# Other rooms and another order for loads and sums in a Fourier-mixing kernel on one core: y's stage, MLP2's begin, chunk 0 and the tail

## The chip, the cores and the metric

The kernel runs on one core of one Trainium2 chip. The metric is device time in microseconds for one execution of the whole program. An execution is also profiled, and the profile gives the start and length of every instruction on each engine: PE (matmuls), PEld (weight loads of PE), DVE (vector), ACT (scalar), POOL and SP, of which SP and POOL here do nothing but start transfers.

## The reference

Four products in a row, all in fp32, on x of 2048 x 512:

```python
xn = _layernorm(x, axis=-1)
a = einsum("bsd,ed->bse", xn, dft_hid_re);  b = einsum("bsd,ed->bse", xn, dft_hid_im)
s = einsum("ts,bse->bte", dft_seq_re, a) - einsum("ts,bse->bte", dft_seq_im, b)
h = einsum("bsd,df->bsf", xn, w1) + b1;  h = relu(h) ** 2
g = silu(einsum("bsf,fd->bsd", h, w2) + b2)
return x + s * g
```

The two Fourier products are made in the other order than written: first along the sequence, then along the hidden dimension.

## The kernel before, in words

**Numbers.** Each fp32 operand is split into a high and a low part: `split_hi` (line 133) on ACT rounds it, `split_lo` (line 136) on DVE subtracts the high part. A product takes three passes of matmuls (`PASSES`): high by high, high by low, low by high. Most products use a scheme of Strassen's kind with seven block products instead of eight. For that, sums of blocks have to be made on DVE before an operand is split (`sums_b`, `sums_a`, `sums_rows`, lines 281 to 299), and results are combined afterwards. An operand so prepared has seven blocks, so one `split_hi` or `split_lo` handles 1792 columns.

**Stages.** They follow one another in PE's order:

- *Chunk 0 and chunk 1* (loops at lines 508 and 560) multiply the normalized x by 256 columns each of the sequence matrices, without the seven-block scheme (`products`, line 367). Each has eight steps j of 24 matmuls of 512 columns. In chunk 0, step j also normalizes the tokens of x_j: statistics (`ln_stats`, `ln_var`), the normalized rows (`ln_xn`) and their split into `xc`. x_j is loaded by `load_x` (line 195), into the room `pq{j // 2 % 2}{j % 2}`.
- *Chunks 2 to 7* (line 593) use the seven-block scheme on x too. Its sums are `sums(g)` (line 245, four instructions on DVE for half of x) and `split_sums` (line 257). They are made aside, in chunk 1: the list `aside` (line 538) holds all these pieces and the first two operands of the hidden matrices, `d0` and `d1`, each piece with a rough cost. `beside(spent)` (line 542) takes pieces from that list in every step of chunk 1 until the cost reaches `ASIDE`.
- *y's stage* (lines 920 and 953) multiplies the result, which lies in DRAM, by the hidden matrices. Its 16 operands are loaded (`y_load`, line 424), summed (`y_sums`) and split (`y_split`). Eight units of two operands each; `Y_SIDE` (line 51) lists what else is made beside each unit.
- *MLP1* (line 995) makes h in 28 units of 84 matmuls; `H_SIDE` (line 63) says what is prepared beside each, among it the first operands of MLP2.
- *MLP2* (line 1037) has 28 steps n = 7 c + p of 42 matmuls of 256 columns. Step n needs the operand `h{n}` (`operand`, line 714) and the weights W2[p]. Each is made in three calls of `go`: load, sums, split. `O_SIDE` (line 94) lists what is called beside the regular calls in the first steps.
- *The tail* (line 1098 on) is the end of MLP2's last part: the products are ordered by block, each output block goes through `silu`, `times` (by s), `plus` (x) or `add_x` (a transfer that adds x), and out.

**What orders the work.** Each engine runs its instructions in the order in which the program lists them; the order above is written out by hand. An engine waits at an instruction until what it needs is there, and all behind it on that engine waits too. SP's queue is the same: a load that waits for its room holds up all loads behind it.

**Rooms.** `buf(tag, ...)` (line 168) gives a tile in a named room. A new tile in a room waits until the last reader of the old one is done. `u` has three rooms that are used in turn; `e`, `wd0`, `wd1` and `pq00` to `pq11` have one each. In MLP1, `wd0` holds W1[6], and `e` holds raw parts of W2. `make_w2` (line 695) loads w6 into `e`; `operand` loads h4, like every fourth, into `wd0`.

**The tail's banks.** C21's last product (k = 4) is made in two halves, in two banks `m4`, after what has to be subtracted was subtracted inside the bank. So only `silu`, `times` and `plus` follow the last matmul. C12's last product (k = 3) is made whole before it.

Of the kernel before, what the change touches and what calls it, by code (L numbers as in the profile page):

```python
# [13 lines left out]
P = 128  # L14
# [7 lines left out]
WARM = 8, 6  # L22
PLAIN = 2

ASIDE = 4.2

REST = NP - 4

# [56 lines left out]
    21: ((), ("h1",), ("w2",)),  # L85
    22: ((), ("h0", "w1"), ()),
    23: ((), ("h1",), ("w3",)),
    24: ((), ("w1",), ("w6", "h2")),
    25: ((), ("w2",), ("h3", "l4")),
    26: ((), ("w2", "w3"), ("l5",)),  # L90
    27: ((), ("w3", "h2"), ()),
}
ACT_PAIR = (4, 6, 8, 10, 12, 14, 16, 18, 21, 25)
O_SIDE = {0: (("h4", "w6"), ("h5",)), 1: ((), ("w6",))}

EPS = 1e-5
HI, LO = 0, 1
# [31 lines left out]
def fnet_gated_kernel(ctx, tc, x, xt, ct, wd, w1, w2, b1, b2, out):  # L129
# [6 lines left out]
    def split_lo(hi, lo, src):  # L136
        nc.vector.tensor_tensor(lo, src, hi.bitcast(F32), op=ALU.subtract)  # L137
# [52 lines left out]
        XC[j] = operand_buf(f"xc{j}", f"xc{j}", 3 if j in TURNED else 1, (7, 2, 256))  # L190
    small = buf("e", [P, 3, 16], "small")

    xr, xn32 = {}, {}

    def load_x(j, hs=slice(0, 2)):

        if j not in xr:
            xr[j] = buf(f"pq{j // 2 % 2}{j % 2}", [P, 2, D], f"x{j}")
        nc.sync.dma_start(xr[j][:, hs], x.rearrange("(h j p) d -> j p h d", h=2, p=P)[j][:, hs])

    def ln_stats(j, h=0):
# [216 lines left out]
        nc.sync.dma_start(x_, PQD[n // 2][:, n % 2])  # L418

    Y_HOME = ("xc3", "xc0"), ("xc4", "xc5"), ("xc6", "xc7")  # L420
    YFIRST = 3
    yop, yraw, WDP = {}, {}, {}

    def y_load(n):
        if n < 2 * NC:
            yraw[n] = buf("u", [P, 8, 256], f"yraw{n}")
            load_pq(n, yraw[n][:, 4:8])

    def y_sums(n):
# [73 lines left out]
    split_hi(*g)  # L503
    for h in range(2):
        products(0, 0, h)
    load_c(0, 3)
    load_x(4)
    for j in range(1, NJ):
        ln_rstd(j)
        for h in range(2):  # L510
            ln_xn(j, h)
            split_hi(*xc_parts(j, h))
        split_lo(*g)
        load_c(*order[j + 3])
        if j + 4 < NJ:
            load_x(j + 4)
        split_lo(*xc_parts(j, 0))
        if j + 1 < NJ:
            ln_stats(j + 1)
            ln_mean(j + 1, 1)  # L520
            ln_var(j + 1, 1)
            ln_root(j + 1)
        split_lo(*xc_parts(j, 1))
        for h in range(2):
            products(0, j, h)
        g = plain_parts(*order[j + 1])
        split_hi(*g)
        if j == 2:
            nc.sync.dma_start(b1s, b1)
            nc.sync.dma_start(b2s, bcast(b2, D))  # L530
    split_lo(*g)


    def run(*names):
        go(*names)
        return 1.6

    aside = chain(sums(0), (split_sums(j) for j in range(ND)), sums(1), (split_sums(j) for j in range(ND, NJ)),
                  (run(v) for v in ("d0", "d0", "d0", "d1", "d1", "d1")))
    accs.append([bank(tag, f"pq1_{tag}") for tag in ("b30", "b31", "b32", "ba")])  # L540

    def beside(spent):
# [9 lines left out]

    plain_out(0)
    plain_out(1)
    beside(0)
    plain_out(2)
    plain_out(3)
    for k in range(2):
# [1 line left out]
    for j in range(NJ - 1):  # L560
        if j == NJ - 4:
            go("d2")
        split(*plain_parts(1, j + 1))
        if j == NJ - 2:
            step_sums(0)
            go("d2")
        load_c(*order[NJ + j + 4])
        if j == 1:
            go("d0", "d1")
        for h in range(2):  # L570
            products(1, j, h)
        beside(split_s1(j - 1) if j else 0)
# [122 lines left out]
    def make_w2(p):  # L695
        if p in (2, 3):
            r, t = (buf(f"pq{p - 2}{i}", [P, 4, 256], f"w2raw{p}_{i}") for i in range(2))
        else:
            e = buf("e", [P, 8, 256], f"w2raw{p}")
            r, t = e[:, 0:4], e[:, 4:8]  # L700
        nc.sync.dma_start(r, w2[p])
        yield
        sums_b(t, r)
        yield
        g = operand_buf(W2_HOME[0 if p in W2_LATE else p], f"w2_{p}", 0)
        for q, src in ((slice(0, 3), r[:, 1:4]), (slice(3, 7), t)) if p in (2, 3) else ((slice(0, 7), e[:, 1:8]),):
            split(g[:, HI, q], g[:, LO, q], src)
        if p in W2_LATE:
            nc.sync.dma_start(W2D[p], g.bitcast(F32))
        else:  # L710
            W2[p] = g
        yield

    def operand(n):

        apart = n in (0, 1, 3)
        if apart:
            x_, t = (buf(f"pq{n % 3}{i}", [P, 4, 256], f"hr{n}_{i}") for i in range(2))
        else:
            e = buf("u" if n % 4 else "wd0", [P, 8, 256], f"hr{n}")  # L720
            x_, t = e[:, 4:8], e[:, 0:4]
        nc.sync.dma_start(x_, HD[divmod(n, NP)])
        yield
        sums_rows(t, x_)
        yield
        g = ready[n] = operand_buf("wd0" if n == NTC * NP - 1 else ("xc6", "xc7", "xc4")[n % 3], f"g{n}", 1)
        for s, src in ((slice(0, 4), t), (slice(4, 7), x_[:, 0:3])) if apart else ((slice(0, 7), e[:, 0:7]),):
            split(g[:, HI, s], g[:, LO, s], src)
        yield
# [190 lines left out]
    for u in range(2):  # L920
        unit = YUnit(u)
        unit.products(1)
        unit.seed("B", "A")
        if u:
            y_split(4)
            y_load(7)
        unit.products(7)
        unit.m7()
        unit.products(6)
        unit.seed("C", "B")  # L930
        y_split(3 + 2 * u, split_hi)
# [12 lines left out]
        if u:  # L944
            y_split(6, split_hi)
        unit.products(3)
        unit.c12()
        if not u:
            y_sums(4)
            y_sums(5)  # L950
    y_sums(7)
    before = None
    for u in range(2, NC):
        n = 2 * u + 2
        unit = YUnit(u)
# [81 lines left out]
    for n in range(NTC * NP):  # L1037
# [74 lines left out]
    silu(e, C11)  # L1112
    for f in (tail - 1, tail):
        rest((6, 7), (f,))
    step(C12, ms[6], C21, ALU.add)
    times(c, e, C11)
    add_x(c, e, C11)
    step(C21, ms[7], C12, ALU.subtract)
    rest((5,), (tail - 1, tail))
    for i in range(2):  # L1120
        nc.vector.tensor_tensor(m4[i][:, w[i]], m4[i][:, w[i]], e[:, C21, w[i]], op=ALU.subtract)
    step(C22, ms[5], C21, ALU.add)
    silu(e, C22)
    step(C12, ms[5], C12, ALU.subtract)
    times(c, e, C22)
    plus(c, e, C22)
    rest((3,))
    put(c, e, C11)
    step(C12, ms[3], C12, ALU.add)
    silu(e, C12)  # L1130
    times(c, e, C12)
    plus(c, e, C12)
    for i, part_ in enumerate((one, two)):
        for f in range(REST, NP):
            outer(m4[i], 4, NP * c + f, (i,))
        nc.scalar.activation(e[:, C21, w[i]], m4[i][:, w[i]], AF.Silu)
        times(c, e, C21, part_)
        plus(c, e, C21, part_)


def _launch(arrays, out_shape):
# [40 lines left out]
```

## Time and profile before

| | us |
|---|---|
| three timed runs | 675.19, 675.82, 680.76 |
| median | 675.82 |
| the profiled execution | 674.92 |
| its span | 673.1 |
| PE busy | 666.6 |
| DVE busy | 597.4 |
| ACT busy | 378.3 |

The span runs from the program's first instruction to its last; the execution's time is 1.8 us longer. A line of a timeline gives start and length in us, engine, line, operation, output and input tile, shape and count; a bracket is the idle time of the engine just before, and what ended it. A row of the windows gives the bounds and length of a stretch, the busy time (and count) of PE, PEld, DVE, ACT and POOL in it, PE's granted clock, and the share and rate of the DMA engines. PE's granted clock is 1.00 wherever a row is shown below.

### The profile page before, as it was taken

The numbers are of one execution on the slowest core, as the hardware profiler recorded it, in microseconds if no ns is written. First come the engines' busy times: TensorE is split into PE (matmuls) and PEld (weight loads), VectorE is DVE, ScalarE is ACT, GpSimd is POOL, SyncE is SP. The second block draws the span as 40 slices with busy tenths as digits, with TensorE's granted clock in tenths as the row PEclk, the third lists the DMA queues.
The fourth block names the chain that finished last, engine by engine and source line by source line (L and its number), as shares of the span: only waits on it lengthen the run. The fifth ranks groups of instructions, "written<-read, shape, count | busy, mean of one in ns | idle before, by whom it ended". The sixth has DMA issues, their size and how long they took to land.

```text
span 673.1 us, 13176 instructions
## 1 busy us (share of the span) xinstructions
PE 666.6 (99%) x5438; PEld 646.9 (96%) x5438; DVE 597.4 (89%) x830; ACT 378.3 (56%) x523; POOL 8.8 (1%) x11
## 2 busy tenths in 40 slices
PE   9999999999999999999999999999999999999997
PEld 6888789999999999999999999999999999999996
DVE  7979888999999999799899989887878789999996
ACT  6845654634444454444465458778778855454451
POOL 0000000000000000000000000000000000101010
PEclk9999999999999999999999999999999999999999
DMA  8635677646556775659588658574856956777775
GB/s 302 215 118 195 214 283 270 218 143 220 203 174 218 258 274 174 249 186 352 187 263 281 218 175 327 190 282 172 298 167 194 349 207 211 190 218 202 209 214 142
DMA packets 51723, 150.82 MB, mean 224 GB/s; under 512 B 4944, under 2 KB 19536, under 8 KB 50256
## 3 DMA queue, kind: packets, MB, share of 16 engines
q1 hardware_dynamic: 43552, 129.28, 56.6%
q10 hardware_dynamic: 6208, 18.88, 7.1%
q0 software_dynamic: 1904, 1.84, 1.9%
q8 instruction: 42, 0.69, 0.4%
q14 instruction: 17, 0.14, 0.1%
HBM read 101.98 MB, written 47.99 MB: 223 GB/s over the span
## 4 chain that ended last, share of the span: by engine, by line
PE 95%; DVE 2%; DMA 2%; issue 0%; ACT 0%; DVEq 0%
PE m L361 34%; PE r_B L752 13%; PE m_o L858 12%; PE r_A L752 9%; PE pq_b L376 8%; PE r_C L752 4%; PE r_D L752 4%; PE m_last L858 4%; PE pq_ba L376 2%; PE pq_bc L376 2%; PE pq_bb L376 2%; DMA hr<-hd 1%; PE warm L482 1%; DVE g L137 0%; DMA out<-z 0%
## 5 line engine op out<-in xcount | busy, mean ns | idle before, releaser
L361 PEld LDWEIGHTS m<-g,xc 128*128 128x128 f32 x2016 | 228.7, 188 | 0.1
L361 PE MATMUL m<-g,xc 128*128 128x256 f32 x2016 | 228.7, 276 | 0.0
L134 ACT ACTIVATE g<-u 128x1792 fp32r<-128x1792 f32 (+2 forms) x65 | 99.0, 1523 | 126.9 <-PE m L361 97.9
L137 DVE TENSOR_TENSOR g<-u,g 128x1792 fp32r<-128x1792 f32 (+2 forms) x65 | 116.8, 1797 | 20.0 <-ACT g L134 19.4
L858 PE MATMUL m_o<-w,g 128*128 128x256 f32 x882 | 101.3, 277 | 0.3 <-DVE g L137 0.2
L858 PEld LDWEIGHTS m_o<-w,g 128*128 128x128 f32 x882 | 100.6, 188 | 0.7 <-DVE g L137 0.7
L134 ACT ACTIVATE g<-hr 128x1792 fp32r<-128x1792 f32 (+2 forms) x31 | 48.1, 1563 | 42.4 <-DVE hr L295 21.0
L752 PE MATMUL r_B<-xT,w 128*128 128x256 f32 x504 | 66.5, 276 | 0.0
L376 PE MATMUL pq_b<-g,xc 128*128 128x512 f32 x240 | 65.6, 392 | 0.0
L752 PEld LDWEIGHTS r_B<-xT,w 128*128 128x128 f32 x504 | 61.4, 188 | 0.0
L137 DVE TENSOR_TENSOR g<-hr,g 128x1792 fp32r<-128x1792 f32 (+2 forms) x31 | 56.7, 1838 | 2.9 <-ACT g L134 2.8
L376 PEld LDWEIGHTS pq_b<-g,xc 128*128 128x128 f32 x240 | 44.7, 188 | 10.8 <-DVE g L137 0.8
L752 PE MATMUL r_A<-xT,w 128*128 128x256 f32 x336 | 42.8, 276 | 0.0
L752 PEld LDWEIGHTS r_A<-xT,w 128*128 128x128 f32 x336 | 40.2, 188 | 0.0
L752 PE MATMUL r_B<-wdp,yg 128*128 128x256 f32 x288 | 35.9, 277 | 0.0
L283 DVE TENSOR_TENSOR u<-u 128x512 f32<-128x512 f32 x48 | 32.9, 685 | 3.1 <-DMA u<-in_ct 3.1
L752 PEld LDWEIGHTS r_B<-wdp,yg 128*128 128x128 f32 x288 | 34.1, 188 | 0.1
L858 PE MATMUL m_last<-w,g 128*128 128x256 f32 x294 | 33.5, 276 | 0.0
L858 PEld LDWEIGHTS m_last<-w,g 128*128 128x128 f32 x294 | 33.4, 188 | 0.0
L137 DVE TENSOR_TENSOR yg<-yraw,yg 128x1792 fp32r<-128x1792 f32 x13 | 26.1, 2017 | 0.3 <-ACT yg L134 0.3
L134 ACT ACTIVATE yg<-yraw 128x1792 fp32r<-128x1792 f32 x13 | 22.2, 1711 | 7.2 <-DVE yraw L292 7.2
L752 PE MATMUL r_D<-xT,w 128*128 128x256 f32 x168 | 23.6, 276 | 0.0
(186 smaller groups left out, 878.0 us busy)
## 6 DMA issues: line engine op xcount, KB each, us to landing
u<-in_ct SPq DMA_DIRECT2D x63, 512.0 KB, 3.9
hd<-h ACTq DMA_DIRECT2D x28, 512.0 KB, 4.0
hr<-hd SPq DMA_DIRECT2D x28, 512.0 KB, 3.7
wdp<-wdd SPq DMA_DIRECT2D x8, 896.0 KB, 7.1
yraw<-pqd SPq DMA_DIRECT2D x13, 512.0 KB, 5.1
pqd<-c SPq DMA_DIRECT2D x6, 1024.0 KB, 6.2
w<-w1d SPq DMA_DIRECT2D x6, 896.0 KB, 9.1
y<-y ACTq DMA_DIRECT2D x8, 512.0 KB, 4.9
```

The costliest lines, as they stand in the source:

```text
L134: nc.scalar.activation(hi, src, AF.Copy)
L137: nc.vector.tensor_tensor(lo, src, hi.bitcast(F32), op=ALU.subtract)
L283: nc.vector.tensor_tensor(t[:, 0:2], r[:, 0:1].to_broadcast([P, 2, 256]), r[:, 1:3], op=ALU.add)
L361: nc.tensor.matmul(ps[:, d], w[:, a_, d * P:(d + 1) * P], halves(mv(b_)), start=first and d == 0 and (a_, b_) == (HI, HI), stop=last and ( ...
L376: nc.tensor.matmul(accs[c][k], w, part[c, j][:, b_, 2 * h:2 * h + 2], start=j == 0 and h == 0 and (a_, b_) == (HI, HI), stop=j == NJ - 1 a ...
L482: nc.tensor.matmul(warm, zeros[:, 0:P], zeros, start=True, stop=True)
L752: nc.tensor.matmul(self.region(REGION[k]), w, mv, start=i == 0 and k in (1, 7), stop=i == len(ops) - 1, skip_group_check=True)
L858: nc.tensor.matmul(m[:, i * 256:(i + 1) * 256], ready[n][:, a_, H_SLOT[a], i * P:(i + 1) * P], W2[p][:, b_, b], start=p == 0 and i == 0 an ...
```

## The change

No matmul is added or taken away; the four places are independent of one another.

1. *Chunk 0 and 1.* `aside` is set up before chunk 0's loop, and the steps j = 5, 6 and 7 each take one piece of it, the first three instructions of `sums(0)`. For their result the room `pq10` has to be free then, so x4 to x7 get other rooms, and x6 and x7 are loaded at j = 3 and 4 instead of 2 and 3. `ASIDE` is 3.6 for 4.2, `beside` begins with 1.5 spent, and the loads for `d0` and `d1` come at j = 0 of chunk 1 for j = 1.
2. *y's stage.* Operand 7 is loaded into `e`, right after operand 6; operands 8, 9 and 10 are loaded one place earlier than before.
3. *MLP2's begin.* w6 goes to `wd0` and h4 to `e`. h4 is loaded beside MLP1's unit 24, where w6 was; w6 is loaded at n = 0, summed at n = 1 and split at n = 2, each one call later. h3's sums take the place of w6's, and h4's that of h3's.
4. *The tail.* `times` and `add_x` of C11 come before the step on C12. C12's last product is made in halves: the left half before C21's two halves, with its `silu`, `times` and `plus`; the right half at the very end, after C12 has been added inside its bank.

```diff
-ASIDE = 4.2
+ASIDE = 3.6
...
-    24: ((), ("w1",), ("w6", "h2")),
+    24: ((), ("w1",), ("h2", "h4")),
...
-O_SIDE = {0: (("h4", "w6"), ("h5",)), 1: ((), ("w6",))}
+O_SIDE = {0: (("w6", "h3"), ("h4", "h5")), 1: ((), ("w6",)), 2: ((), ("w6",))}
...
+    X_ROOM = "pq00", "pq01", "pq10", "pq11", "pq00", "pq01", "pq11", "pq00"
-            xr[j] = buf(f"pq{j // 2 % 2}{j % 2}", [P, 2, D], f"x{j}")
+            xr[j] = buf(X_ROOM[j], [P, 2, D], f"x{j}")
...
-    YFIRST = 3
+    YFIRST, Y_APART = 3, 7
...
-            yraw[n] = buf("u", [P, 8, 256], f"yraw{n}")
+            yraw[n] = buf("e" if n == Y_APART else "u", [P, 8, 256], f"yraw{n}")
...
-        if j + 4 < NJ:
-            load_x(j + 4)
+        if j in (1, 3, 4):
+            load_x({1: 5, 3: 6, 4: 7}[j])
...
         split_lo(*xc_parts(j, 1))
+        if j >= NJ - 3:
+            next(aside)
         for h in range(2):
             products(0, j, h)
...
-    beside(0)
+    beside(1.5)
...
-        if j == 1:
+        if j == 0:
             go("d0", "d1")
...
-            e = buf("e", [P, 8, 256], f"w2raw{p}")
+            e = buf("wd0" if p == NP - 1 else "e", [P, 8, 256], f"w2raw{p}")
...
-            e = buf("u" if n % 4 else "wd0", [P, 8, 256], f"hr{n}")
+            e = buf("e" if n == 4 else "u" if n % 4 else "wd0", [P, 8, 256], f"hr{n}")
...
         if u:
             y_split(4)
-            y_load(7)
+            y_load(8)
...
-        y_load(6 + 2 * u)
+        y_load(9 if u else 6)
+        if not u:
+            y_load(Y_APART)
...
-        y_load(n + 3)
+        y_load(n + (4 if u == 2 else 3))
...
-        y_load(n + 4)
+        if u > 2:
+            y_load(n + 4)
...
-        go(f"h{n + 3}")
+        if n > 1:
+            go(f"h{n + 3}")
...
-    step(C12, ms[6], C21, ALU.add)
     times(c, e, C11)
     add_x(c, e, C11)
+    step(C12, ms[6], C21, ALU.add)
     step(C21, ms[7], C12, ALU.subtract)
...
+    step(C12, ms[5], C12, ALU.subtract)
     step(C22, ms[5], C21, ALU.add)
     silu(e, C22)
-    step(C12, ms[5], C12, ALU.subtract)
+
+    def kept(m, k, i):
+        for f in range(REST, NP):
+            outer(m, k, NP * c + f, (i,))
+
+    kept(ms[3], 3, 0)
+    step(C12, ms[3], C12, ALU.add, w[0])
+    silu(e, C12, one)
+    nc.vector.tensor_tensor(ms[3][:, w[1]], ms[3][:, w[1]], e[:, C12, w[1]], op=ALU.add)
     times(c, e, C22)
     plus(c, e, C22)
-    rest((3,))
+    times(c, e, C12, one)
+    plus(c, e, C12, one)
     put(c, e, C11)
-    step(C12, ms[3], C12, ALU.add)
-    silu(e, C12)
-    times(c, e, C12)
-    plus(c, e, C12)
-    for i, part_ in enumerate((one, two)):
-        for f in range(REST, NP):
-            outer(m4[i], 4, NP * c + f, (i,))
-        nc.scalar.activation(e[:, C21, w[i]], m4[i][:, w[i]], AF.Silu)
-        times(c, e, C21, part_)
-        plus(c, e, C21, part_)
+    for k, to, i in ((4, C21, 0), (4, C21, 1), (3, C12, 1)):
+        m = m4[i] if k == 4 else ms[3]
+        part_ = slice(i, i + 1)
+        kept(m, k, i)
+        nc.scalar.activation(e[:, to, w[i]], m[:, w[i]], AF.Silu)
+        times(c, e, to, part_)
+        plus(c, e, to, part_)
```

More of the change, by code (lines that the diff above doesn't have):

```diff
@@ L505, in fnet_gated_kernel, with run @@
         products(0, 0, h)
+    def run(*names):
+        go(*names)
+        return 1.6
+    aside = chain(sums(0), (split_sums(j) for j in range(ND)), sums(1), (split_sums(j) for j in range(ND, NJ)),
+                  (run(v) for v in ("d0", "d0", "d0", "d1", "d1", "d1")))
     load_c(0, 3)
@@ L531, in fnet_gated_kernel @@
     split_lo(*g)
[L534 to L539, printed above, removed]
     accs.append([bank(tag, f"pq1_{tag}") for tag in ("b30", "b31", "b32", "ba")])
```

## The prediction

> **What bounds the kernel now.** I read the page first (busy time, then the chain that ended last), then the stage windows, one unit of PE's work to a window, then the timelines of DVE, ACT and PE wherever a window was longer than its neighbours.
>
> ```profile
> span 673.1 us, 13176 instructions
> PE 666.6 (99%) x5438; PEld 646.9 (96%) x5438; DVE 597.4 (89%) x830; ACT 378.3 (56%) x523; POOL 8.8 (1%) x11
> PE 95%; DVE 2%; DMA 2%; issue 0%; ACT 0%; DVEq 0%
> ```
>
> PE is busy 99% of the span and the chain is PE for 95% of it. The diff adds and removes no matmul, so it can win only where PE waits or after PE's last matmul. Two stages have such places. The first is chunk 1, one row for each step j = 2 to 5 (24 matmuls):
>
> ```profile
> 61.98:67.43 5.45, 5.45 (x25) 4.51 (x24) 4.47 (x5) 2.80 (x5) 0.00 (x0) 1.00 0.72 277
> 67.43:73.09 5.66, 5.66 (x25) 4.43 (x24) 5.59 (x9) 4.93 (x8) 0.00 (x0) 1.00 0.27 93
> 73.09:78.69 5.60, 5.60 (x25) 4.43 (x24) 5.53 (x10) 3.73 (x6) 0.00 (x0) 1.00 0.73 273
> 78.69:84.13 5.44, 5.44 (x25) 4.50 (x24) 3.40 (x4) 1.37 (x2) 0.00 (x0) 1.00 0.98 285
> ```
>
> After the bounds and the length come the busy times of PE, PEld, DVE and ACT. A step takes 5.44 us; j = 3 and j = 4 take 5.66 and 5.60, and there DVE is full (5.59, 5.53). PE loses 0.22 + 0.16 = **0.38 us** to a late `split_lo`. The second place is the start of MLP2, one row for each n = 2 to 5 (42 matmuls):
>
> ```profile
> 543.20:547.96 4.76, 4.76 (x44) 4.76 (x43) 3.20 (x6) 4.61 (x4) 0.00 (x0) 1.00 0.84 305
> 547.96:553.24 5.28, 5.21 (x44) 5.01 (x43) 5.21 (x6) 1.62 (x2) 0.00 (x0) 1.00 0.03 11
> 553.24:558.48 5.24, 5.06 (x45) 4.86 (x44) 5.10 (x8) 2.18 (x2) 0.00 (x0) 1.00 0.36 117
> 558.48:563.24 4.76, 4.76 (x45) 4.76 (x44) 4.69 (x6) 1.71 (x1) 0.00 (x0) 1.00 0.59 204
> ```
>
> n = 3 and n = 4 take 5.28 and 5.24 instead of 4.76: 0.52 + 0.48 = **1.00 us** lost. What comes before, on DVE (a bracket is the idle time before an instruction and what ended it), then one row of ACT and one of the chain:
>
> ```profile
> 535.68 0.69 DVE L283 TENSOR_TENSOR w2raw<-w2raw 128x512 f32<-128x512 f32 x1
> ...
> 541.65 0.69 DVE L289 TENSOR_TENSOR hr<-hr 128x512 f32<-128x512 f32 x1
> ...
> 544.75 0.69 DVE L289 TENSOR_TENSOR hr<-hr 128x512 f32<-128x512 f32 x1 [1.49 <-DMA hr<-hd]
> ...
> 546.28 2.08 DVE L137 TENSOR_TENSOR g<-hr,g 128x1024 fp32r<-128x1024 f32 x2
> 548.29 2.02 DVE L137 TENSOR_TENSOR w<-w2raw,w 128x1792 fp32r<-128x1792 f32 x1
> 550.22 0.68 DVE L289 TENSOR_TENSOR hr<-hr 128x512 f32<-128x512 f32 x1
> ...
> 551.74 2.02 DVE L137 TENSOR_TENSOR g<-hr,g 128x1792 fp32r<-128x1792 f32 x1
> 553.68 0.69 DVE L289 TENSOR_TENSOR hr<-hr 128x512 f32<-128x512 f32 x1
> ```
> ```profile
> 543.35 1.80 ACT L134 ACTIVATE g<-hr 128x1024 fp32r<-128x1024 f32 x2 [2.16 <-DVE hr L295]
> ```
> ```profile
> 535.90 8.76 DMA hr<-hd
> ```
>
> In the program's order these are: sums of w6 (535.68), sums of h3 (541.65), sums of h4 (544.75), `split_lo` of h3 (546.28), of w6 (548.29), sums of h5 (550.22), `split_lo` of h4 (551.74), sums of h6 (553.68). h4's load goes into `wd0`, so it leaves only when PE has finished with W1[6] (535.90), and lands 8.76 us later. DVE is in order and sits 1.49 us at h4's sums with h3's `split_lo` behind them; PE needs h3's low part at 547.96 and h4's at 553.24, and both come late.
>
> **The end.** DVE, ACT and PE of the last 15 us, and the last stores:
>
> ```profile
> 658.71 0.69 DVE L1104 TENSOR_TENSOR z<-m_last,z 128x512 f32<-128x512 f32 x1 [1.02 <-ACT z L1110]
> 660.67 0.69 DVE L1104 TENSOR_TENSOR z<-m_last,z 128x512 f32<-128x512 f32 x1 [1.28 <-PE m_last L858]
> ...
> 662.60 0.76 DVE L1121 TENSOR_TENSOR m_last<-m_last,z 128x256 f32<-128x256 f32 x2
> 663.27 1.28 DVE L1104 TENSOR_TENSOR z<-m_last,z 128x512 f32<-128x512 f32 x2
> ...
> 667.38 0.69 DVE L908 TENSOR_TENSOR z<-z,fin 128x512 f32<-128x512 f32 x1 [0.70 <-ACT z L904]
> 668.10 0.69 DVE L913 TENSOR_TENSOR z<-z,fin 128x512 f32<-128x512 f32 x1
> ...
> 669.96 0.42 DVE L913 TENSOR_TENSOR z<-z,fin 128x256 f32<-128x256 f32 x1
> ```
> ```profile
> 668.15 0.38 ACT L1136 ACTIVATE z<-m_last 128x256 f32<-128x256 f32 x1 [0.54 <-PE m_last L858]
> ```
> ```profile
> 654.81 13.31 PE L858 MATMUL m_last<-w,g 128*128 128x256 f32 x116
> ```
> ```profile
> out<-z SPq DMA_DIRECT2D x2, 128.0 KB, 1.7
> ```
>
> PE ends at 654.81 + 13.31 = 668.12, ACT's last `silu` at 668.53. DVE ends at 670.38, for it is behind: it waited 1.28 us for PE (660.67) and 0.70 us for the whole C12's `silu` (667.38), and the whole C12 is still being added at 668.10.
>
> **The change part by part.**
>
> *Chunk 0.* Three of the four instructions of `sums(0)` move from the start of chunk 1 into DVE's work for j = 5, 6, 7. One takes 1.22 us:
>
> ```profile
> 41.52 1.22 DVE L137 TENSOR_TENSOR g<-u,g 128x1024 fp32r<-128x1024 f32 x1
> ...
> 48.08 1.22 DVE L254 TENSOR_TENSOR s<-xn 128x1024 f32<-128x1024 f32 x1
> ```
> ```profile
> 41.38 1.13 ACT L134 ACTIVATE xc<-xn 128x512 fp32r<-128x512 f32 x2
> ```
>
> They hide behind PE's steps. A step is 5.44 us; counted back from 61.98, j = 7 starts at 61.98 - 3 x 5.45 = 45.63. Before j = 7 two of the three have run, 2 x 1.22 = 2.44 us: its `g` low part ends at 42.74 + 2.44 = 45.18, and PE wants it after four matmuls (0.9 us), at 46.5; its first `xc` high part ends about 42.0 + 2.44 = 44.4, wanted at 45.63. So 1.2 to 1.3 us are to spare and this costs 0. Were the cover gone, each such instruction would cost up to its 1.22 us. x6 and x7 are loaded one step later, into other rooms whose readers are done, two steps (10.9 us) before use, which is more than the 8.76 us that a load of the same 512 KB took above: 0. In chunk 1 the list `aside` then stands four instructions ahead, and the limit 3.6 for 4.2 takes work out of j = 2 to 4, the fullest steps. One `split_sums` costs DVE 0.9 us:
>
> ```profile
> 67.94 2.69 DVE L137 TENSOR_TENSOR xc<-xn,xc 128x768 fp32r<-128x768 f32 x3
> ```
>
> Added up for DVE, j = 2 then has 0.42 + 4 x 0.9 + 1.2 = 5.2 us and j = 3 and 4 a little over 4 each, all under 5.44, and by that count `split_lo` comes 1.1 to 2.2 us before PE asks. Gain **0.38**, bounds 0 and 0.38. `go("d0","d1")` at j = 0 puts two loads on SP one step earlier, behind the store of `plain`; the next load on SP has a step's room: 0.
>
> *y's stage.* yraw7 goes into `e`, yraw 8 to 10 are loaded one place earlier. That takes away waits such as this one, on DVE:
>
> ```profile
> 350.55 0.69 DVE L289 TENSOR_TENSOR yraw<-yraw 128x512 f32<-128x512 f32 x1 [0.57 <-DMA yraw<-pqd]
> ```
> ```profile
> 390.56 0.42 DVE L765 TENSOR_TENSOR y<-r_C,y 128x256 f32<-128x256 f32 x1 [0.88 <-PE r_C L752]
> ...
> 400.34 0.42 DVE L762 TENSOR_TENSOR y<-r_B,y 128x256 f32<-128x256 f32 x1
> ```
>
> But PE doesn't wait there: DVE is ahead again and waits for PE at 390.56. If PE is held anywhere here, it is at 400.34, where DVE comes without a pause from the ten microseconds of work that follow 390.56; the diff leaves that work alone. Gain 0. On SP the load into `e` waits for the store of the last chunk from `e`, with room before the next load. Were that store late, y's loads behind it would be too; DVE's 0.9 us at 390.56 bounds what it absorbs. Bounds -0.3 and +0.3.
>
> *MLP2's begin.* h4 is loaded into `e` about 16 us earlier, w6 takes `wd0` and leaves at 535.90 in its place; w6's sums and split move back by a round, h3's sums take their place at 535.68, h4's that of h3's at 541.65. So the 1.49 us wait goes. What is late next is h3's `split_lo`, which follows ACT's (543.35, first half done about 544.4): DVE starts at 544.45 instead of 546.28. From there, with the distances between starts above: h3 2.01 to 546.46, w6's sums 1.52 (like 550.22 to 551.74) to 547.98, h5's sums 1.52 to 549.50, h4's `split_lo` 1.94 to 551.44 (wanted at 552.7), w6's 1.94 to 553.38, where h6's sums start, 0.30 earlier than now. h5's low part ends about 557.0, wanted at 557.5 + 0.2. So both stalls go, 1.00 us. The narrowest place is then n = 8:
>
> ```profile
> 570.09 2.02 DVE L137 TENSOR_TENSOR g<-hr,g 128x1792 fp32r<-128x1792 f32 x1
> ```
>
> h8's low part ends at 572.11 - 0.30 = 571.8; PE, 1.00 us earlier, starts n = 8 at 558.48 + 3 x 4.76 - 1.00 = 571.76 and wants it two matmuls (0.23 us) later. DVE is nearly the bound, so I take **0.9**, bounds 0 and 1.0.
>
> *The tail.* C12's product (k = 3) is made in halves; its left half comes first of the four last half-products, its right half last. `times` of C11 moves ahead of the step that waits for PE at 660.67, so DVE fills that 1.28 us; the last whole `silu` (0.70 us of waiting) is gone. Start to start a 512-wide step takes about 0.61 us, a 256-wide one 0.34, and a dependent one its own time (0.69, 0.42) + 0.03. By hand from 659.40: `times` C11 660.09, C12 660.7, C21 661.4, m4 662.1 and 662.5, C12 662.8, C22 663.4, C12's left 664.07 (PE's left half ends 668.12 - 3 x 1.36 = 664.04), the add into its right half 664.4, C22 664.8 and 665.5, C12's left 666.1 and 666.6, C21 666.9, 667.4, 667.7 and 668.1, free at 668.56. The last half's `silu` ends at 668.53, so `times` starts about 668.57 and `plus` ends at 669.44 instead of 670.38; the store (1.7 us) follows as now. Gain **0.94**, bounds 0.4 and 1.0. Splitting costs three instructions more: 2 x 0.34 - 0.61 = 0.07 us each if independent, 2 x 0.42 - 0.69 = 0.15 if not.
>
> The Trainium skill, VectorE: DVE Perf Modes, section "The TRN2 errata", speaks against this part: an SBUF-sourced instruction pays a fixed latency whatever its size, so many small ones cost more than one large, and it advises 512 elements or more. [...]
>
> **The sum.** The profiled execution took 674.92 us, its span 673.1 with 1.8 around it. 674.92 - 0.38 - 0.9 - 0.94 = 672.7. The three timed runs are 675.19, 675.82 (the median) and 680.76, so the profiled execution lies 0.9 under the median; the middle of 674.92, 675.19 and 675.82 is 675.3, and 675.3 - 2.2 gives **673.1 us**. A 1% difference (6.8 us), about what a measurement of this kernel can tell from no change, is three times as much.
>
> **Rivals.**
>
> *DVE becomes MLP2's bound.* The 0.3 us that DVE gains is all that PE can keep; the stall returns at n = 5 or n = 8. For it: DVE is 5.21 of 5.28 busy, and my margin at n = 8 is 0.2 us. Against: from n = 9 on PE waits nowhere now. 675.3 - 0.38 - 0.94 - 0.3 = 673.7; with nothing gained there, 674.0.
>
> *The moved sums don't fit.* If `sums(0)` holds j = 6 or 7 up by what j = 3 and 4 gain and the tail keeps only 0.4, the change doesn't do what it says: 675.3 - 0.9 - 0.4 = 674.0; with MLP2's stalls left as well, 674.9.
>
> *w6's load is late (slower).* w6's sums now stand in DVE's queue ahead of h5's sums and h4's `split_lo`, and its load starts at 535.90 amid heavy traffic. It has until 546.46, 10.6 us; h4's load from that place took 8.76. Larger loads, started ten microseconds before, took this:
>
> ```profile
> DMA to landing us min/median/max: 8.7/11.4/14.1
> ```
>
> At 14.1 it lands at 550.0, 3.6 us late; less h4's margin of 1.3 PE loses 2.3, then about 0.6 more at n = 5, and none of the 1.00 is a gain on top: 675.3 - 0.38 - 0.94 + 1.9 = 675.9, and a landing after 16 us would give 677.8. It decides from 13.5 us on. Against: 512 KB like h4's, in h4's place, with the same neighbours.
>
> **How the numbers follow.** Forecast 0.56; DVE the bound 0.17; moved sums 0.12; w6 late 0.10; the rest 0.05. The forecast's own range is 672.0 to 674.2. To leave no more than 2 in 10 out, and as single runs differ by 0.9 us, I take 671.9 to 675.9. Faster by over 1% would need more than all that PE waits: 0.02. Slower by over 1% needs a wait of 9 us, such as a queue blocked by a room that isn't free: 0.04. Within 1%: 0.94.
>
> **What would show it.** Windows of 5.44 us for every step of chunk 1 and of 4.76 for n = 3, 4 and 8; no DVE wait for `hr` at h4's sums; DVE's last instruction about 1.3 us after PE's last matmul (now 2.3). A chunk-0 step over 5.5 us, a stall at n = 4 to 8 ended by DVE, or DVE waiting for w6's load would prove a step wrong.

## The result, and the profile after

| | before | after |
|---|---|---|
| median of the timed runs, us | 675.68 (14 runs, 674.81 to 680.76) | 673.36 (14 runs, 672.62 to 673.87) |
| ratio | | 0.9952, 95% interval 0.9934 to 0.9969 |
| the profiled execution, us | 674.92 | 673.52 |
| its span, us | 673.1 | 671.7 |

The forecast was 673.1 us with a range of 671.9 to 675.9, and within 1%. The time came out at 673.36. The profile's page of after:

```profile
span 671.7 us, 13186 instructions
PE 665.4 (99%) x5438; PEld 646.5 (96%) x5438; DVE 597.3 (89%) x833; ACT 379.0 (56%) x524; POOL 8.8 (1%) x11
```

The matmuls are the same 5438, DVE has the three additional instructions of the split, and PE is 1.2 us less busy: in these records a PE that waits inside a run of matmuls counts as busy (the step of 5.66 us of before has 5.66 us of PE), so a lost stall shows up as less busy time. The windows of after, for j = 2 to 4 of chunk 1 and for n = 2, 3, 4 and 8 of MLP2 (columns as in the prediction):

```profile
62.26:67.71 5.45, 5.45 (x25) 4.51 (x24) 5.40 (x6) 4.28 (x6) 0.00 (x0) 1.00 0.35 107
67.71:73.16 5.45, 5.45 (x25) 4.51 (x24) 5.38 (x9) 2.87 (x5) 0.00 (x0) 1.00 0.37 132
73.16:78.61 5.45, 5.45 (x26) 4.51 (x24) 4.48 (x7) 2.84 (x4) 0.00 (x0) 1.00 0.77 250
543.77:548.53 4.76, 4.76 (x44) 4.76 (x43) 4.62 (x9) 2.86 (x2) 0.00 (x0) 1.00 0.83 296
548.53:553.29 4.76, 4.76 (x44) 4.76 (x43) 4.76 (x4) 2.24 (x2) 0.00 (x0) 1.00 0.07 25
553.29:558.05 4.76, 4.76 (x44) 4.76 (x43) 4.62 (x8) 1.72 (x1) 0.00 (x0) 1.00 0.50 149
572.33:577.09 4.76, 4.76 (x44) 4.76 (x43) 4.69 (x7) 2.24 (x2) 1.33 (x1) 1.00 0.56 190
```

5.66, 5.60, 5.28 and 5.24 have become 5.45, 5.45, 4.76 and 4.76. Both stalls are gone as forecast. DVE is still full in j = 2 and 3 (5.40, 5.38) and n = 3 (4.76 of 4.76): it has hardly less to do there, but does it in an order in which PE's operand is ready in time. MLP2's begin on DVE and on ACT:

```profile
542.22 0.68 DVE L290 TENSOR_TENSOR hr<-hr 128x512 f32<-128x512 f32 x1
...
543.74 2.09 DVE L137 TENSOR_TENSOR g<-hr,g 128x1024 fp32r<-128x1024 f32 x2
545.75 0.69 DVE L284 TENSOR_TENSOR w2raw<-w2raw 128x512 f32<-128x512 f32 x1
...
548.80 2.02 DVE L137 TENSOR_TENSOR g<-hr,g 128x1792 fp32r<-128x1792 f32 x1
...
569.07 2.02 DVE L137 TENSOR_TENSOR g<-hr,g 128x1792 fp32r<-128x1792 f32 x1
```
```profile
541.93 1.80 ACT L134 ACTIVATE g<-hr 128x1024 fp32r<-128x1024 f32 x2 [0.17 <-PE m_o L861]
```

No wait is left between h4's sums (542.22) and h4's low part (548.80), and w6's sums (545.75) did not wait for w6's load. h8's low part ends at 571.09 and is wanted at 572.33 + 0.23 = 572.56: the margin at the narrowest place is **1.5 us**, not 0.2. The row of ACT says why, and the section on the prediction comes back to it.

The end, on PE, DVE and ACT:

```profile
651.78 15.92 PE L861 MATMUL m_last<-w,g 128*128 128x256 f32 x139
...
659.67 0.69 DVE L911 TENSOR_TENSOR z<-z,fin 128x512 f32<-128x512 f32 x1 [0.70 <-ACT z L907]
660.28 1.48 DVE L1111 TENSOR_TENSOR z<-m_last,z 128x512 f32<-128x512 f32 x2
...
667.73 0.38 ACT L1150 ACTIVATE z<-m_last 128x256 f32<-128x256 f32 x1 [0.97 <-PE m_last L861]
...
668.17 0.42 DVE L911 TENSOR_TENSOR z<-z,fin 128x256 f32<-128x256 f32 x1
668.62 0.42 DVE L916 TENSOR_TENSOR z<-z,fin 128x256 f32<-128x256 f32 x1
```

PE ends at 651.78 + 15.92 = 667.70 and DVE at 669.04, 1.34 us later (2.26 before). The wait of 1.28 us for PE is gone.

These three places add up to 0.4 + 1.0 + 0.9 = 2.3 us, but the profiled span is only 1.4 us shorter. Two stalls of after take the rest, on DVE near 282 us in chunk 6 and on PE in chunk 0's first step:

```profile
282.22 0.69 DVE L284 TENSOR_TENSOR u<-u 128x512 f32<-128x512 f32 x1 [2.23 <-DMA u<-in_ct]
```
```profile
12.53 0.39 PE L377 MATMUL pq_bc<-g,xc 128*128 128x512 f32 x1
13.12 0.73 PE L377 MATMUL pq_b<-g,xc 128*128 128x512 f32 x2 [0.20 <-ACT xc L134]
```

After the first PE stands at 285.5, and it loses 0.7 us there in all, 0.6 more than in before; the second costs 0.3 us more. 2.3 - 0.6 - 0.3 = 1.4. Whether they belong to the change is asked below (the changed kernel once more).

### The profile page after: what moved, and what is told of

Its sections match the earlier page's. It is cut to its first block, busy times and chain, and to the rows that moved or that the text cites. A ratio compares the mean times of both kernels' runs of the same rounds, so it can differ in the third digit from the quotient of the medians.

```text
span 671.7 us, 13186 instructions
## 1 busy us (share of the span) xinstructions
PE 665.4 (99%) x5438; PEld 646.5 (96%) x5438; DVE 597.3 (89%) x833; ACT 379.0 (56%) x524; POOL 8.8 (1%) x11
## 4 chain that ended last, share of the span: by engine, by line
PE 94%; DVE 2%; DMA 2%; ACT 1%; issue 0%; SPq 0%; DVEq 0%; ACTq 0%
PE m L362 32%; PE m_o L861 15%; PE r_B L755 13%; PE r_A L755 9%; PE pq_b L377 8%; PE r_C L755 4%; PE r_D L755 4%; PE m_last L861 4%; PE pq_ba L377 2%; PE pq_bc L377 1%; PE pq_bb L377 1%; DMA u<-in_ct 1%; DMA x<-in_x 1%; DVE g L137 1%; DVE z L1111 0%; DVE z L911 0%
```

## Experiments

Every kernel was timed beside the kernel before. "Ratio" is the time over that of the kernel before, with its 95% interval. The kernel before had medians of 675.82, 675.77 and 675.57 us in the three groups of runs (35 runs each).

### One part alone, four kernels

The kernel before with one of the four parts of the change's diff and nothing else. The tail (part 4), of which the last lines are:

```diff
-    for i, part_ in enumerate((one, two)):
-        for f in range(REST, NP):
...
+    for k, to, i in ((4, C21, 0), (4, C21, 1), (3, C12, 1)):
...
+        kept(m, k, i)
```

> The kernel before with the tail's edit alone. Theory (the parts are independent, each worth what PE or the end loses at its own place): 0.94 us faster, DVE's last instruction about 1.3 us after PE's last matmul instead of 2.3, PE's windows elsewhere as before. Rival (the three more instructions of the halves stand at the end of DVE's queue): 0.4 to 0.6 us faster, and DVE without a wait for PE in the last 5 us.

MLP2's begin (part 3):

```diff
+O_SIDE = {0: (("w6", "h3"), ("h4", "h5")), 1: ((), ("w6",)), 2: ((), ("w6",))}
...
+            e = buf("wd0" if p == NP - 1 else "e", [P, 8, 256], f"w2raw{p}")
```

> The kernel before with the edit at MLP2's begin alone. Theory: n = 3 and n = 4 take 4.76 us, 0.9 to 1.0 us faster, and n = 8 keeps 4.76. Rival (DVE is MLP2's bound): the stall comes back at n = 5 or n = 8 and only 0.3 us stay.

Chunk 0 and 1 (part 1):

```diff
+ASIDE = 3.6
...
+        if j >= NJ - 3:
+            next(aside)
```

> The kernel before with the edit in chunks 0 and 1 alone. Theory: all steps of chunk 1 take 5.44 us, 0.38 us faster. Rival: the lead is lost again in chunk 6, where the profile of the changed kernel shows a stall of 0.65 us at 285 us behind a late load of ct, since that load's landing is set by the DMA and not by PE: 0.0 us, and a stall of about 0.4 us at 285 us.

y's stage (part 2):

```diff
+            yraw[n] = buf("e" if n == Y_APART else "u", [P, 8, 256], f"yraw{n}")
```

> The kernel before with the edit in y's stage alone. Theory: no change (within 0.2 us); DVE no longer waits for yraw's loads, and waits for PE the longer at 390 us. Rival: the earlier loads let DVE arrive earlier at 400 us too, and PE's stall there goes: 0.3 us faster.

| part alone | median, us | ratio | at its place in the profile |
|---|---|---|---|
| tail | 675.18 | 0.9974 [0.9947, 1.0002] | DVE ends 1.35 us after PE (2.26) |
| MLP2's begin | 674.91 | 0.9974 [0.9954, 0.9994] | n = 3, 4 and 8 take 4.76 |
| chunk 0 and 1 | 675.94 | 1.0009 [0.9985, 1.0033] | j = 3 and 4 take 5.45 |
| y's stage | 676.26 | 1.0008 [0.9988, 1.0029] | in y's stage PE stands only near 400 us, as before |

Each part does at its place what was expected of it. The two last medians show nothing of it, because the timed runs of these kernels, like those of the kernel before, are of two kinds: most lie under 677 us, and some of them 4 to 5 us higher, up to 681. Without those above 677 us (a limit that I chose after seeing them) the kernel before has a median of 675.6, the tail alone 674.4, chunk 0 and 1 675.1 and y's stage 675.6, and MLP2's begin alone (674.9) has none above: -1.2, -0.5, 0 and -0.7, about the size of the forecast terms. The profiled executions of chunk 0 and 1 and of y's stage are among the higher ones. What they show is told in the last section.

With chunk 0 and 1 alone the stall at 285 us costs 0.15 us, so the rival that the lead of 0.38 us is lost there does not hold.

y's stage alone changes no time. What it does is seen elsewhere: in the profile of MLP2's begin alone, which has y's stage as before, one of y's loads was late, and PE stood.

```profile
371.39 0.69 DVE L289 TENSOR_TENSOR yraw<-yraw 128x512 f32<-128x512 f32 x1 [1.68 <-DMA yraw<-pqd]
```
```profile
375.33 1.63 PE L752 MATMUL r_B<-wdp,yg 128*128 128x256 f32 x12 [0.64 <-DVE y L762]
```

Of eight profiles with y's stage as before, one has such a stall (0.9 us in all); of six with the changed one, none has. That is too few to show that the edit prevents it.

### MLP2: order without rooms, w6 later, more work for DVE

The order alone: w6 stays in `e` and h4 in `wd0`; only h4's sums and w6's split come later.

```diff
-O_SIDE = {0: (("h4", "w6"), ("h5",)), 1: ((), ("w6",))}
+O_SIDE = {0: (("h4", "w6"), ("h5",)), 1: ((), ("h4",)), 2: ((), ("w6",))}
...
-        go(f"h{n + 3}")
+        if n != 1:
+            go(f"h{n + 3}")
```

> The kernel before with the order of MLP2's first steps changed and no room: h4 still goes to wd0 and is loaded at 535.9 us, but its sums come behind h3's split_lo instead of ahead of it, and w6's split comes one step later. Theory (the loss was a wait in DVE's queue ahead of h3's split_lo, not the late load itself): DVE has 1.2 us at h3's split_lo anyway, h4 has landed by then, n = 3 and n = 4 take 4.76 us, 0.9 to 1.0 us faster like the edit with rooms. Rival (h4's late load sets the time): a stall of 0.3 us or more stays at n = 4.

The changed kernel with w6's load one call later, so behind other loads on SP:

```diff
-O_SIDE = {0: (("w6", "h3"), ("h4", "h5")), 1: ((), ("w6",)), 2: ((), ("w6",))}
+O_SIDE = {0: (("h3",), ("h4", "h5")), 1: (("w6",), ("w6",)), 2: ((), ("w6",))}
```

> The changed kernel with w6's load put one place later on SP, behind those of h5 and h6, so that it starts at about 542 and lands at about 548 us, 1.5 us after DVE comes to w6's sums. It tries the rival of the prediction that w6's load is late. Theory: n = 4 keeps 4.76 (1.3 us of margin), n = 5 or n = 8 lose 0.3 to 0.8 us. Second theory, from the traces so far: after a stall in this place PE can go on at 118 ns a matmul instead of 113 until the next wait, which costs 4.5 us over the thousand matmuls left; then a part of the runs lies 4 to 5 us higher. Rival: no loss at all.

The changed kernel with h5's sums made twice, 1.5 us more for DVE:

```diff
-        sums_rows(t, x_)
+        for _ in range(2 if n == 5 else 1):
+            sums_rows(t, x_)
```

> The changed kernel with h5's sums made twice (1.5 us more for DVE, ahead of h4's split_lo; the result is the same). It asks how near DVE is to being MLP2's bound. Theory: PE stalls at n = 4, n = 5 or n = 8, together 1.2 to 1.5 us, since DVE has no room to catch up before n = 9; and if a stall can set PE to 118 ns a matmul for the rest, a part of the runs lies 4 to 5 us higher. Rival (DVE has room): under 0.5 us and no run 4 us higher.

| | median, us | ratio |
|---|---|---|
| order alone | 674.90 | 0.9976 [0.9960, 0.9991] |
| w6 later | 674.99 | 0.9980 [0.9961, 0.9998] |
| DVE + 1.5 us | 673.59 | 0.9968 [0.9947, 0.9988] |

The windows of n = 8 with the order alone, of n = 4, 5 and 8 with w6 later, and of n = 8 with more work for DVE:

```profile
572.38:577.53 5.15, 5.06 (x44) 4.86 (x43) 5.08 (x8) 2.90 (x4) 0.34 (x1) 1.00 0.41 129
```
```profile
552.82:558.12 5.30, 5.21 (x45) 5.01 (x44) 5.23 (x6) 1.63 (x2) 0.00 (x0) 1.00 0.29 102
558.12:563.35 5.23, 5.05 (x44) 4.85 (x43) 5.09 (x8) 2.18 (x2) 0.00 (x0) 1.00 0.38 113
572.87:578.22 5.35, 5.04 (x44) 4.84 (x43) 5.28 (x8) 3.11 (x4) 0.34 (x1) 1.00 0.47 147
```
```profile
572.33:577.32 4.99, 4.99 (x45) 4.85 (x43) 4.92 (x8) 2.75 (x4) 0.34 (x1) 1.00 0.39 124
```

*Order alone.* n = 3 and 4 are free of stalls without any new room; 0.39 us comes back at n = 8, which was not expected. By the windows the order gives most of the gain (1.0 - 0.39 = 0.6 us), the rooms the rest; the medians (674.90, and 674.91 for the whole part) don't tell the two apart. Its DVE and ACT, beside the rows of after above, show where the rooms' share comes from:

```profile
545.07 2.09 DVE L137 TENSOR_TENSOR g<-hr,g 128x1024 fp32r<-128x1024 f32 x2 [1.19 <-ACT g L134]
```
```profile
543.98 1.80 ACT L134 ACTIVATE g<-hr 128x1024 fp32r<-128x1024 f32 x2 [2.16 <-DVE hr L295]
```

Here h3's sums stay where they were, ACT's `split_hi` of h3 waits 2.16 us for them and starts at 543.98, and DVE waits 1.19 us for ACT and starts h3's low part at 545.07. In after h3's sums stand one place earlier, ACT starts at 541.93 as soon as PE has freed its room, and DVE at 543.74. PE stands at the same point in both (n = 2 at 543.83 and 543.77), so DVE has 1.3 us more.

*w6 later.* This makes the slower rival come true:

```profile
548.18 0.69 DVE L284 TENSOR_TENSOR w2raw<-w2raw 128x512 f32<-128x512 f32 x1 [2.81 <-DMA w2raw<-in_w]
```

DVE waits 2.81 us for w6, and PE loses 0.54 + 0.47 + 0.59 = 1.6 us at n = 4, 5 and 8, which the timed runs agree with (674.99 against 673.36). A wait of 1.5 us that spares n = 4 was expected; DVE came to w6's sums earlier than I had counted (545.4 instead of 546.46), so it waited longer, and n = 4 was hit too. The mechanism is as the prediction had it, but in the change itself the load leaves at 536.47 and takes 8.5 us, so it lands at 545.0, 0.8 us before DVE asks:

```profile
536.47 0.33 SPq L704 DMA_DIRECT2D w2raw<-in_w  x1
```
```profile
w2raw<-in_w SPq DMA_DIRECT2D x1, 512.0 KB, 8.5
```

*More work for DVE.* 1.5 us more costs 4.99 - 4.76 = 0.23 us, all at n = 8, and nothing at n = 3 to 5; 1.2 to 1.5 us were expected. So DVE had about 1.3 us to spare, and the rival that DVE becomes the bound was further off than its chance said.

### The tail: its two halves

Only `times` and `add_x` of C11 moved ahead:

```diff
-    step(C12, ms[6], C21, ALU.add)
     times(c, e, C11)
     add_x(c, e, C11)
+    step(C12, ms[6], C21, ALU.add)
```

> The kernel before with one edit of the tail: times and add_x of C11 ahead of the step on C12, no halves. Theory: DVE uses 0.6 us of its 1.28 us wait, everything behind moves up, its last instruction ends 0.6 us earlier after PE's last matmul (1.7 us instead of 2.3): 0.6 us faster. Rival (the whole C12's silu and product set the end): 0.0 to 0.2 us.

Only C12's last product in halves, `times` of C11 where it was:

```diff
-    rest((3,))
...
+    kept(ms[3], 3, 0)
+    step(C12, ms[3], C12, ALU.add, w[0])
+    silu(e, C12, one)
...
+    for k, to, i in ((4, C21, 0), (4, C21, 1), (3, C12, 1)):
```

> The kernel before with one half of the tail's edit: C12's last product in halves, the right half at the very end; times and add_x of C11 stay where they were, behind the step on C12. Theory (both halves of the edit are needed, and they add up): moving C11's times ahead alone took 0.38 us off the end; the halves alone then take 0.5 to 0.6, so DVE ends about 1.7 us after PE's last matmul (2.26 before, 1.35 with the whole edit). Rival (the halves do it all): DVE ends 1.35 to 1.4 after PE. Rival (a fixed price for each small instruction eats it): DVE ends 2.0 us after PE or later. Time 0.5 us under the kernel before.

The last matmuls of PE and the last instruction of DVE, with `times` moved, then with the halves:

```profile
653.74 15.35 PE L858 MATMUL m_last<-w,g 128*128 128x256 f32 x134
...
667.96 0.69 DVE L908 TENSOR_TENSOR z<-z,fin 128x512 f32<-128x512 f32 x1 [0.70 <-ACT z L904]
...
670.54 0.42 DVE L913 TENSOR_TENSOR z<-z,fin 128x256 f32<-128x256 f32 x1
```
```profile
653.76 15.24 PE L858 MATMUL m_last<-w,g 128*128 128x256 f32 x133
...
661.56 0.69 DVE L1104 TENSOR_TENSOR z<-m_last,z 128x512 f32<-128x512 f32 x1 [1.28 <-PE m_last L858]
...
670.31 0.42 DVE L913 TENSOR_TENSOR z<-z,fin 128x256 f32<-128x256 f32 x1
```

PE ends at 669.09 and 669.00, DVE at 670.96 and 670.73: 1.87 and 1.73 us later, a gain of 0.39 and 0.53 against the 2.26 before. They add up to the whole part's 0.92. `times` alone was expected to bring 0.6 and brought 0.39, since the wait for the whole C12's `silu` (0.70 us at 667.96) is still there and takes back part of what DVE had won. Medians: 675.39, ratio 0.9980 [0.9958, 1.0001], and 675.01, ratio 0.9999 [0.9980, 1.0017]; neither can be told from the kernel before by its time alone, so the verdict rests on the rows.

### Chunk 1: the limit alone

```diff
-ASIDE = 4.2
+ASIDE = 3.6
...
-        if j == NJ - 4:
+        if j == NJ - 3:
```

> The kernel before with only the limit of the side work in chunk 1 lowered from 4.2 to 3.6, and the load for d2 asked for one step later (j = 5); no sum moves into chunk 0. Theory (the limit is what frees chunk 1, the moved sums only make room for what the limit pushes back): windows of j = 3 and j = 4 come down to 5.45 from 5.66 and 5.60, 0.3 to 0.4 us gained, and the work that is pushed back shows as a fuller DVE at j = 5 to 7 without a stall there. Rival (chunk 1 has too much DVE work at any limit unless three sums are made in chunk 0): one step of j = 3 to 7 still holds more than 5.45 us of DVE work, and a stall of 0.2 us or more stays somewhere in chunk 1; gain 0 to 0.2.

The windows of j = 2 to 5:

```profile
61.98:67.43 5.45, 5.45 (x26) 4.51 (x25) 4.50 (x6) 2.61 (x4) 0.00 (x0) 1.00 0.86 310
67.43:72.88 5.45, 5.45 (x26) 4.51 (x25) 5.42 (x8) 4.43 (x7) 0.00 (x0) 1.00 0.18 55
72.88:78.33 5.45, 5.45 (x26) 4.51 (x25) 5.35 (x9) 2.83 (x4) 0.00 (x0) 1.00 0.62 212
78.33:83.78 5.45, 5.45 (x26) 4.52 (x25) 3.86 (x5) 3.06 (x4) 0.00 (x0) 1.00 1.01 362
```

The stalls are gone with two lines and no move into chunk 0. So the three sums that the change makes in chunk 0, with their rooms and loads, are not needed to free chunk 1; the limit is enough, with d2's load one step later, which was not tried apart. Two rows of DVE in the kernel before show one thing that the limit does:

```profile
65.51 0.96 DVE L137 TENSOR_TENSOR xc<-xn,xc 128x768 fp32r<-128x768 f32 x1 [0.91 <-ACT xc L134]
66.46 1.22 DVE L137 TENSOR_TENSOR g<-u,g 128x1024 fp32r<-128x1024 f32 x1
```

Before, a piece of the side work that waits 0.91 us for ACT stands ahead of the `split_lo` of j = 3, which ends at 67.68 for a step that begins at 67.43. With the lower limit that piece comes one step later: the `split_lo` starts at 63.46, and the same wait of 0.91 us stands behind it, at 67.06. It is the pattern of MLP2's begin once more. Median 675.04, ratio 0.9997 [0.9981, 1.0014]: 0.4 us can't be told by the time.

### Two more moves, and the changed kernel once more

The changed kernel, with a sum taken out of y's last unit (PE stood 0.35 us near 400) and with p0's loads earlier (the stall at 285.5):

```diff
-    (6, 1): ("y1",), (6, 3): ("y1", "p0"), (6, 4): ("p0",),
+    (6, 1): ("y1",), (6, 2): ("p0",), (6, 3): ("y1", "p0"),
...
-    (("x0", "x0", "x1", "x1", "V2"), ("V4", "V3", "x2", "x2")),
+    (("x0", "x0", "x1", "x1", "V2"), ("V4", "x2", "x2")),
...
-    0: ((), ("V2", "x2"), ("x3",)),
+    0: ((), ("V2", "x2", "V3"), ("x3",)),
```

> The changed kernel with two further moves: the second sum V3 made beside y's last unit goes into MLP1's first unit, so that the last combining steps of y's stage reach DVE earlier (PE stood 0.35 us near 400 us there), and two loads of p0 in chunk 6 are issued one or two steps earlier (PE stood 0.65 us at 285.5 behind a load that landed 0.2 us late). Theory (both waits were DVE's order and a load's late start): both stalls are gone, nothing new appears, and the median is 0.3 to 0.9 us under the changed kernel's, about 672.7. Rival (the stall near 400 is the length of the chain from PE's last result over ACT and DVE back to PE, and the one at 285 is how long the loads take at that traffic): one or both stay, 673.0 to 673.5.

The changed kernel unaltered:

> The changed kernel once more, unaltered. Theory (the stalls of 0.36 us at 12.5 and 0.65 us at 285.5 in its first profile are the spread of transfer times): they change in size in this profile, while the windows of 5.45 and 4.76 us and the 1.35 us at the end stay within 0.05; median 673.1 to 673.7, and no run above 676, for no stall is left at MLP2's begin after which PE could go on at 118 ns a matmul. Rival (the second group of runs is chance and belongs to every kernel): two or three of its runs lie 3 to 6 us higher.

The two moves brought nothing: 673.28 us, ratio 0.9957 [0.9940, 0.9974], beside 672.97, ratio 0.9961 [0.9948, 0.9974], of the unaltered kernel on the same chip. Both stalls went from where they were, and others came nearby. On DVE at 272.8 and on PE at 415.3, with the two moves; then on PE in the changed kernel, at the same place in the program:

```profile
272.81 0.69 DVE L284 TENSOR_TENSOR u<-u 128x512 f32<-128x512 f32 x1 [1.60 <-DMA u<-in_ct]
```
```profile
415.33 1.93 PE L755 MATMUL r_B<-xT,w 128*128 128x256 f32 x12
```
```profile
415.78 1.52 PE L755 MATMUL r_B<-xT,w 128*128 128x256 f32 x12
```

In both kernels the `u` load that is late has a load of p0 (896 KB) under way beside it: it takes 7.1 us (6.9 in the changed kernel) where its neighbours take 3.4 to 5.6, and PE loses 0.5 us. The moved load seems only to choose which `u` load it hits; no run leaves p0's load out. And the twelve matmuls at 415.33 take 1.93 us for 1.52: PE, which did not stand at 401, now runs into MLP1's first units, where DVE needs 5.32 us for a unit (it adds to h at 405.13, 410.45 and 415.77) and PE 4.76. (A unit of MLP1 has 42 matmuls, not the 84 of the description of the kernel.)

The changed kernel's second profile has the same windows and the same 1.34 us at the end; its stall at 285 costs 0.5 us for 0.7, that at 12.5 is as in the first. Whether these two stalls are the change's stays partly open. The one at 285 costs 0 to 0.4 us in the profiles of the eight kernels with chunk 0 and 1 as before, and 0.15, 0.15, 0.25, 0.5 and 0.7 in the five that have part 1 or the whole change (without the two moves). At 12.5 the interval between two matmuls is 0.27 to 0.39 us in the eight, and 0.29 to 0.59 in the six with part 1, though their instructions are the same up to there. That speaks for the spread of transfer times as most of it; a share of 0.1 to 0.2 us each is not excluded. No run of the kernel lies above 674.4. By itself that says little against the rival that the higher runs belong to every kernel, for on this chip only 2 of 35 runs of the kernel before were above 677 us; the count over all kernels, in the last section, says more.

## Why the prediction was right

**Chunk 1, -0.38: right in size, and right in one reason of two.** The windows show the whole gain, and the steps j = 5 to 7 of chunk 0 take 5.44 us, as in before (j = 0 and 1 were over 5.5 us in before too, and j = 0 has the stall at 12.5). The count of DVE's work came out too. It has to be read in DVE's order, from one step's `split_lo` to the next, and not in PE's windows, where j = 3 (5.38) holds two microseconds that j = 2 had left over:

```profile
64.67 1.22 DVE L137 TENSOR_TENSOR g<-u,g 128x1024 fp32r<-128x1024 f32 x1
...
69.62 1.22 DVE L137 TENSOR_TENSOR g<-u,g 128x1024 fp32r<-128x1024 f32 x1
```

That is 4.95 us for j = 2 where 5.2 was counted. What failed is "the list `aside` then stands four instructions ahead" as a reason: at chunk 1's first step five of its pieces are done and four in before, and after j = 1 twelve and thirteen. The gain does not need the sums to leave chunk 1; the limit, the other reason, gives it.

**y's stage, 0: right.** The median of the runs under 677 us is 675.6 both times. The stall that the edit might prevent was in no profile that I had then.

**MLP2's begin, -0.9: right, but the margin was mis-sized.** The step that failed is "h3's `split_lo`, which follows ACT's (543.35 ...): DVE starts at 544.45". I took ACT's start as fixed. Its row, quoted in the prediction itself, says otherwise: `[2.16 <-DVE hr L295]`, it waited for h3's sums, and these are moved ahead by the change. In after it starts at 541.93 and DVE at 543.74. The prediction's 544.45, shifted by the 0.63 us that PE was later in the profile of the order alone, is 545.08, and that is what the order alone gave (545.07), where h3's sums were not moved. So "DVE is nearly the bound" described a kernel without the new rooms; with them DVE has 1.5 us at n = 8, and PE loses 0.2 us when 1.5 us of work are added to DVE. The same error hid a cost: DVE also comes to w6's sums earlier, at 545.75, so w6's load had 0.8 us to spare and not the 1.8 of the prediction (10.6 less 8.76). The gain itself is smaller on the average than the 1.00 us of the one profile of before: the profiles of seven kernels with this stage unchanged show 0.56 to 1.12 us at n = 3 and 4. h4's load takes 8.3 to 8.8 us in them and DVE waits 1.06 to 1.49 us for it; the shortest wait goes with the smallest loss.

**The tail, -0.94: measured 0.92.** The halves at the end cost what the rows said. The rule of the Trainium skill, VectorE: DVE Perf Modes, section "The TRN2 errata", by which many small instructions cost more than one large, agrees with the rows (0.15 us for a dependent pair of halves, 2 x 0.42 - 0.69); but the trace shows no such loss at the end, because the three instructions that were added do not all stand behind PE's last matmul. What stands there is one `silu`, the rest of C21's `plus`, and one `times` and one `plus` of 256 columns; in before, DVE still had the whole C12's `plus` and both halves of C21 to do (668.10 on). One miss stayed hidden: the hand count let `times` of C11 start at 659.40, though its own row waits 0.70 us for `silu`; DVE catches up before the left half of C12 is there.

**The sum.** The terms in the profile are 2.3 us, as forecast (2.2). The profiled executions show 1.4 of it, the timed runs under 677 us 2.1 to 2.6 (675.5 and 675.6 against 673.36 and 672.97), the medians 2.3 and 2.6, and the ratio, which counts the higher runs of before too, 3.2 us. Right size, then, but that the median came within 0.3 us of the forecast is partly luck: the two stalls of after, at 12.5 and 285.5, are in no term of the sum. The higher runs are the subject of the last section.

**The rivals.** "DVE the bound" and "w6's load late" did not happen, but each was made by an experiment, and PE waited at the steps that the prediction had named (and at n = 8 too with w6 late), by other amounts. "The moved sums don't fit" is refuted by the windows.

## What to carry to other kernels

Before a start time is carried over from the old trace into a forecast, read the bracket of that row: an instruction that waited for something which the change moves will itself move. Where PE waited here for an in-order engine that was nearly full, the order of that engine's work was worth more than its amount, so look for a wait that stands ahead of what PE needs. Try the cheapest edit (here a limit) before work is moved between stages. And here a stall behind a load that was late by a few tenths was not removed by moving the neighbouring load; it came back at another one.

## What the hardware showed that was not expected

**PE goes on at two paces.** A step of 42 matmuls in MLP2 takes 4.76 us, 113.3 ns each. In the profiles of chunk 0 and 1 alone and of y's stage alone, PE goes on more slowly after its stall at n = 4, to the end of the kernel. Windows of n = 3, 4 and 6 and of a stretch of 40 us, with chunk 0 and 1 alone; then of n = 6 and the same stretch with MLP2's begin alone:

```profile
548.60:553.69 5.09, 5.04 (x44) 4.85 (x43) 5.02 (x6) 1.47 (x2) 0.00 (x0) 1.00 0.04 14
553.69:559.24 5.55, 5.21 (x45) 5.01 (x43) 5.41 (x8) 2.33 (x2) 0.00 (x0) 1.00 0.37 111
564.18:569.13 4.95, 4.95 (x44) 4.95 (x43) 4.74 (x9) 3.28 (x4) 0.00 (x0) 1.00 0.61 194
...
600.00:640.00 40.00, 40.00 (x342) 40.00 (x341) 36.89 (x49) 20.97 (x22) 2.44 (x2) 1.00 0.75 216
```
```profile
563.64:568.40 4.76, 4.76 (x44) 4.76 (x43) 4.55 (x9) 3.29 (x4) 0.00 (x0) 1.00 0.68 215
...
600.00:640.00 40.00, 40.00 (x355) 40.00 (x354) 38.57 (x51) 19.46 (x21) 2.44 (x2) 1.00 0.73 210
```

4.95 us a step is 117.9 ns a matmul, and 342 matmuls pass in 40 us instead of 355. PE waits for nothing there, DVE is less busy, and the granted clock is 1.00 in both. Over the thousand matmuls that follow, 4.5 ns each are 4.5 us, and the spans of these two profiles are 677.9 and 677.2. The Trainium skill, TensorE: Matmul & The Clock Gate, Part 1, states a gap of N / 2.4 GHz and some 2.5 ns for back-to-back matmuls; at 256 columns that would be 109 ns (an estimate from that page). Neither pace here is that, and no run shows what makes the one or the other.

The slower pace also comes in short stretches, in all profiles, and it can end without a wait. From about 397 us 38 matmuls or more go at 118 ns with no stall ahead of them; in eight profiles this ends near 401, in the other six PE goes on so to about 413 (140 matmuls), and there it ends with no stall. In the changed kernel the pace follows the stall at 285.5:

```profile
287.00:295.00 8.00, 8.00 (x70) 8.00 (x69) 7.65 (x10) 2.89 (x3) 0.00 (x0) 1.00 0.38 129
```

Before has 73 matmuls in the same stretch. The slower pace lasts for some 80 matmuls there, so about half of the 0.7 us lost at 285.5 is pace and not waiting. It is the same at n = 3 of before, where some 0.2 of the 0.52 us are pace.

The stretch to the end fits the higher timed runs. Of 119 runs of the kernel before, 22 lie above 677 us, nearly all at 679 to 681; of the 72 runs of the kernels that keep the stalls at n = 3 and 4, 14. Of the 60 runs of kernels without them (the change twice, with the two moves, MLP2's begin alone, and the order alone, which has 0.39 us at n = 8), none lies above 676.7. The kernel with more work for DVE, whose last stall is at n = 8 with 840 matmuls to go, has three of twelve runs at 676.5 to 677.8, up to 4 us above its others; the kernel with w6 later, with stalls at n = 4, 5 and 8, has only one of twelve above 677 us, at 677.7. So after such a stall there seems to be a chance of about one in five that PE goes on at the slower pace to the end. It was not the same throughout: counted over the kernel before and the kernels that keep these stalls, 28 of 118 runs beside the first eight experiments lie above 677 us, and 5 of 59 beside the last four, on another chip. That the two profiles change pace after the stall is shown. That the unprofiled runs at 679 us are the same thing is inferred from their number and size, and what decides the pace, and how long it lasts, stays open. If it is so, the change is worth more on the average than its 2.3 us of stalls, for it also takes away the place after which the slower pace could last to the end: the means of all runs differ by 3.3 and 2.7 us.
